# How E and F reach a fused attention and MLP-mixer kernel on one core: two loads moved from GpSimd to SyncE, with their casts on ScalarE and VectorE

## The chip, the cores and the metric

The kernel runs on one core of one Trainium2 chip. The metric is device time in microseconds (us) of one execution. Beside the times there is one profiled execution: each instruction on TensorE (PE, with its weight loads as PEld), VectorE (DVE), ScalarE (ACT) and GpSimd (POOL), the DMA instructions that POOL and SyncE (SP) issue, and the packets that the core's 16 DMA engines moved.

## The reference

```python
k_proj = einsum('ks,bhsd->bhkd', E, k)          # q, k, v: 8 batches, 8 heads, 1024 rows, 64 columns
v_proj = einsum('ks,bhsd->bhkd', F, v)          # E, F: 64 x 1024
scores = softmax(q @ k_proj^T / sqrt(64))       # 1024 x 64 for each head
x = (scores @ v_proj), heads side by side       # 8 x 1024 x 512
h = relu(x^T @ w_tok1) @ w_tok2                 # 1024 -> 256 -> 1024, over the rows
u = x + h^T
out = u + relu(u @ w_ch1) @ w_ch2               # 512 -> 1536 -> 512
```

All inputs and the output are f32 in DRAM. On the chip the products run in bf16. Everything that uses k or v needs E or F first, so these two matrices (256 KB each in f32) stand at the head of the computation.

## The kernel before, in words

The program treats the eight batches one after another and mixes the instructions of neighbouring batches. Each step has a short name, and a list `ORDER`, written out by hand, gives the order in which the steps are written to the engines; each engine then runs its own instructions in that order. `ON_DVE` names the copies that go to DVE; the others go to ACT.

Loads are issued by POOL (`nc.gpsimd.dma_start`), because they cast f32 to bf16 on the way. POOL's instructions also run in the order in which they stand, so a load waits for all that POOL has to do ahead of it. The order at the start is: E (L197) and F (L198) into the two halves of the tile `EF_sb`, 64 partitions each; then, for each of the four pairs of heads of batch 0, a load of k, of q and of v (`load`, L165, 256 KB each as bf16), with `make_identity` (a memset and a select on POOL, masks.py:197 and 199) after the v load of the first pair; then `wt1` (L206), `wt2` (L207), the channel weights (L191, L195) and q, k and v of batch 1.

On PE the start is as follows. `busy(c_ps, 8)` runs eight matmuls on a tile of zeros (L226); their product isn't used. Step `EF` (`eft`, L228 to L232) turns `EF_sb` with eight transposes, which need `EF_sb` and `ident`, and DVE copies the result to `EFT`. Step `KP.0` multiplies `EFT` with k of the first pair of heads (L240), `QT.0` transposes q (L395), `VP.0` multiplies with v (L245), and so on for the pairs 1, 2 and 3, in the order that the first lines of `ORDER` give:

```python
EF KP.0 Ka.0 W1 KT.0 Ba.0 Bd.0 QT.0 KP.1 QC.0 VP.0 Ka.1 S1.0 QT.1 KT.1 QC.1 VP.1 lv2 Bd.1 Ba.1
Vd.0 KP.2 S0.0 Va.0 E1.0 Vd.1 O1.0 Ka.2 QT.2 Va.1 KT.2 S0.1 E0.0 S1.1 E1.1 QC.2 Ba.2 Bd.2 O0.0
```

`W1` is three more matmuls on zeros, and `KP.1`, `KP.2`, `KP.3` and `VP.3` begin with four, two, two and three matmuls of the same kind (`FILL`, L431). S and E are scores and exponentials, O is the product with v, M and N are the two token products (L464, L477). After about 35 us the channel products of batch 0 follow (L532), and from batch 1 on they are done with seven products of half-size blocks where eight would be plain (L600, L655).

SP issues the transposing DMAs of q and u (L178, L362) and the stores of the output (L676, L680) from the f32 tiles `o1` and `o2`, of two buffers each. It issues nothing in the first 70 us.

## Time and profile before

| What | Value |
|---|---|
| time, three runs | 430.47, 430.73, 430.92 us |
| profiled execution | 430.72 us, of which the trace spans 428.9 us from its first to its last instruction |
| PE busy in the span | 416.0 us (97%) |
| DVE, ACT, POOL busy | 302.0, 202.4, 205.7 us |
| granted TensorE clock | 0.999 |
| moved by POOL's DMA queue | 29.63 MB as they land (bf16), 43.9% of 16 engines' span |
| moved by SP's DMA queue | 30.42 MB, 29.6% |

The busy share of PE is an average over the whole span, and it counts matmuls that wait in the pipeline. The stage that the change touches is the first of the profile's 40 slices, each of 10.7 us. The bytes of a load that casts are counted as they land, so 205 GB/s of landed bf16 stand for 410 GB/s read from DRAM.

### The profile page before, as it was taken

How to read it: one execution, taken by the hardware profiler on the slowest of the kernel's cores; microseconds unless marked ns; L12 is line 12 of the kernel's file. 1: busy time of each engine (PE TensorE's matmuls, PEld its weight loads, DVE VectorE, ACT ScalarE, POOL GpSimd, SP SyncE). 2: the span in 40 equal slices, each digit the busy share in tenths (PEclk: the TensorE clock that was granted, in tenths of full speed). 3: DMA queues.
4: the chain of work that ended last, by engine and by line, in shares of the span. 5: the costliest groups of instructions: out<-in, count | busy, mean ns of one | idle time of the engine just before them, and what ended most of it. 6: DMA issues, size and time to landing. Idle time of an engine off the chain costs nothing.

```text
span 428.9 us, 7732 instructions
## 1 busy us (share of the span) xinstructions
PE 416.0 (97%) x3066; PEld 271.0 (63%) x3066; DVE 302.0 (70%) x509; ACT 202.4 (47%) x360; POOL 205.7 (48%) x150
## 2 busy tenths in 40 slices
PE   6799999999999999999999999999999999999995
PEld 3486456765478644785467744786458854785585
DVE  2575568768836878867768777777779766947862
ACT  1446684167553556234753365334652356215621
POOL 8350024135563547552565645635456626654652
PEclk9999999999999999999999999999999999999999
DMA  8999999879996999943999279364914320342014
GB/s 128 207 202 206 207 205 183 208 128 223 194 124 172 171 222 184 178 81 70 253 164 203 114 132 160 66 169 113 147 36 105 92 99 2 60 140 98 2 50 147
DMA packets 89332, 60.53 MB, mean 141 GB/s; under 512 B 55760, under 2 KB 84944, under 8 KB 89296
## 3 DMA queue, kind: packets, MB, share of 16 engines
q0 software_dynamic: 29360, 29.63, 43.9%
q1 hardware_dynamic: 59936, 30.42, 29.6%
q8 instruction: 24, 0.39, 0.4%
q14 instruction: 12, 0.10, 0.1%
HBM read 59.24 MB, written 16.78 MB: 177 GB/s over the span
## 4 chain that ended last, share of the span: by engine, by line
PE 91%; DVE 4%; DMA 2%; POOL 2%; issue 0%; ACT 0%; DVEq 0%; ACTq 0%; POOLq 0%
PE be L655 19%; PE be L600 17%; PE ga L655 9%; PE ga L600 8%; PE h_ps L341 6%; PE u_ps L357 5%; PE g_ps L532 5%; PE al L655 4%; PE al L600 4%; PE ou_ps L294 4%; PE kv_ps L240 3%; PE sco L281 3%; DMA q_sb<-in_q_dram 2%; DVE S L524 1%; PE u_ps L477 1%; PE h_ps L464 1%
## 5 line engine op out<-in xcount | busy, mean ns | idle before, releaser
L564 ACT ACTIVATE K<-be 128x512 f32<-128x512 f32 x116 | 65.7, 598 | 66.2 <-PE be L655 39.4
L655 PEld LDWEIGHTS <-g 128*128 128x128 bf16 x768 | 74.5, 98 | 16.2 <-issue 1.0
L655 PEld LDWEIGHTS <-S 128*128 128x128 bf16 x576 | 55.9, 98 | 11.7 <-issue 0.4
L286 ACT ACTIVATE attnT<-sco 128x512 bf16<-128x512 f32 x56 | 33.5, 598 | 50.8 <-PE sco L281 50.7
L600 PEld LDWEIGHTS <-wc 128*128 128x128 bf16 x336 | 32.1, 98 | 36.1 <-DVE g L606 0.4
L691 POOL TENSOR_TENSOR K<-K,u_sb 128x512 f32<-128x512 f32 x16 | 19.0, 1185 | 68.5 <-ACT K L564 68.5
L655 PE MATMUL be<-wc,g 128*128 128x256 bf16 x384 | 48.5, 273 | 0.6 <-DVE g L522 0.6
L564 ACT ACTIVATE K<-ga 128x512 f32<-128x512 f32 x58 | 33.0, 601 | 33.6 <-PE ga L655 29.9
L301 DVE TENSOR_TENSOR x_sb<-ou_ps,rdn 128x512 bf16<-128x512 f32 x64 | 44.3, 692 | 2.2
L600 PE MATMUL be<-uT,wc 128*128 128x512 bf16 x168 | 44.7, 379 | 0.0
L360 DVE TENSOR_TENSOR u_sb<-u_ps,x_sb 128x512 bf16<-128x512 f32 x56 | 37.1, 684 | 9.4 <-PE u_ps L357 8.9
L600 PEld LDWEIGHTS <-uS 128*128 128x128 bf16 x252 | 24.0, 98 | 25.7
L606 DVE CUSTOM_DVE_ANT_0 g<-be,K 128x512 bf16<-128x512 f32 x42 | 27.5, 688 | 16.8 <-PE be L600 16.6
L518 POOL TENSOR_TENSOR S<-g 128x1024 bf16<-128x1024 bf16 x7 | 14.8, 2121 | 47.0 <-DVE g L606 47.0
L522 POOL TENSOR_TENSOR g<-g 128x1024 bf16<-128x1024 bf16 x13 | 28.9, 2226 | 14.8 <-DVE S L518 14.6
L639 ACT ACTIVATE g<-be 128x512 bf16<-128x512 f32 x42 | 23.8, 597 | 25.7 <-PE be L600 25.7
L606 DVE CUSTOM_DVE_ANT_0 g<-al,K 128x512 bf16<-128x512 f32 x42 | 27.7, 688 | 10.7 <-PE al L600 10.4
L701 POOL TENSOR_TENSOR K<-K,u_sb 128x512 f32<-128x512 f32 x16 | 20.0, 1247 | 30.0 <-ACT K L564 30.0
L357 PE MATMUL u_ps<-R_sb,wt 128*128 128x512 bf16 x112 | 31.0, 379 | 0.3 <-DVE u_sb L360 0.3
L300 DVE RECIPROCAL rdn<-ou_ps 128x8 f32<-128x8 f32 x64 | 13.1, 205 | 25.8 <-PE ou_ps L294 25.4
L341 PE MATMUL h_ps<-x_sb,wt 128*128 128x512 bf16 x112 | 29.9, 379 | 0.0
L524 POOL TENSOR_TENSOR S<-g,S 128x1024 bf16<-128x1024 bf16 x13 | 28.4, 2185 | 0.9 <-ACT K L564 0.7
(101 smaller groups left out, 777.1 us busy)
## 6 DMA issues: line engine op xcount, KB each, us to landing
out_dram<-o SPq DMA_DIRECT2D x30, 512.0 KB, 3.0
q_sb<-in_q_dram POOLq DMA_DIRECT2D x7, 1024.0 KB, 13.0
k_sb<-in_k_dram POOLq DMA_DIRECT2D x7, 1024.0 KB, 11.5
v_sb<-in_v_dram POOLq DMA_DIRECT2D x7, 1024.0 KB, 13.4
wc<-in_moe_w_ch_dram POOLq DMA_DIRECT2D x4, 384.0 KB, 14.3
wc<-in_moe_w_ch_dram POOLq DMA_DIRECT2D x2, 768.0 KB, 27.7
k_sb<-in_k_dram POOLq DMA_DIRECT2D x4, 256.0 KB, 7.0
q_sb<-in_q_dram POOLq DMA_DIRECT2D x4, 256.0 KB, 7.6
```

What stands on the lines that cost most here:

```text
L286: nc.scalar.activation(out=at, in_=sco, func=ACT.Exp, scale=scale)
L301: nc.vector.tensor_tensor(out=st["x", b][:, :, h * D : (h + 1) * D].rearrange("p (b k) d -> p b k d", b=2), in0=ov[:, :, :, 0:D], in1=rdn[ ...
L341: nc.tensor.matmul(st["h", b], wt1[:, s, t * P : (t + 1) * P], st["x", b][:, s, :], start=(s == 0), stop=(s == SC - 1),)
L357: nc.tensor.matmul(u_ps, wt2[:, t, s::SC], st["R", b][:, t, :], start=(t == 0), stop=(t == TC - 1))
L360: nc.vector.tensor_add(out=st["u", b][:, s, :], in0=u_ps, in1=st["x", b][:, s, :])
L522: eng.tensor_sub(out=a21, in0=a11, in1=a21)
L524: eng.tensor_sub(out=s4, in0=a12, in1=s2)
L564: nc.scalar.activation(out=t, in_=x, func=ACT.Copy)
L600: nc.tensor.matmul(acc, l[:, dc, i * P : (i + 1) * P], r[:, :, dc, :], start=start and dc == 0, stop=stop and dc == 1, skip_group_check=True,)
L606: nc.vector._custom_dve(TENSOR_ADD_SAT, out=o, in0=x, in1=y, s0=3.0e38, s1=0.0)
L639: nc.scalar.activation(out=g_part(b, i + e, 1, 1, 0)[:, 0], in_=be[e], func=ACT.Relu)
L655: nc.tensor.matmul(acc[:, e * HF : (e + 1) * HF], l[:, lc + c, l0 + (2 * j + e) * P : l0 + (2 * j + e + 1) * P], r[:, rc + c, r0 : r0 + HF ...
```

## The change

E and F are no longer loaded by POOL with a cast. SP loads them as f32 into a new tile `EF_in`, which takes a buffer of the tag `o1`. ACT then casts columns 0 to 511 into `EF_sb` and DVE columns 512 to 1023. POOL's first instruction of the kernel's body is now the load of k of the first pair of heads, followed by q, then `make_identity`, then v and all the rest in the old order. On ACT the cast stands ahead of all its other work, behind the load of its function table; on DVE it stands after the four memsets and ahead of the copy to `EFT`. On PE nothing is added, removed or moved.

```diff
-    nc.gpsimd.dma_start(out=EF_sb[0:KP], in_=E)
-    nc.gpsimd.dma_start(out=EF_sb[KP:P], in_=F)
+    EF_in = work.tile([P, S], F32, tag="o1", name="EF_in", bufs=2)
+    nc.sync.dma_start(out=EF_in[0:KP], in_=E)
+    nc.sync.dma_start(out=EF_in[KP:P], in_=F)
     for hp in range(HP):
         hs = slice(2 * hp, 2 * hp + 2)
         for name, src in ((("k", k), ("q", q), ("v", v))):
             load(0, name, src, hs)
-        if hp == 0:
-            make_identity(nc, ident)
+            if (hp, name) == (0, "q"):
+                make_identity(nc, ident)
...
     busy(c_ps, 8)
+    nc.scalar.activation(out=EF_sb[:, 0 : S // 2], in_=EF_in[:, 0 : S // 2], func=ACT.Copy)
+    nc.vector.tensor_copy(out=EF_sb[:, S // 2 : S], in_=EF_in[:, S // 2 : S])
```

## The prediction

> **What bounds the kernel now.** The page's slices come first, to see which stage differs from the rest:

> ```profile
> ## 2 busy tenths in 40 slices
> PE   6799999999999999999999999999999999999995
> ...
> GB/s 128 207 202 206 207 205 183 208 128 223 194 124 172 171 222 184 178 81 70 253 164 203 114 132 160 66 169 113 147 36 105 92 99 2 60 140 98 2 50 147
> ```

> PE is full from slice 3 on. Only in slices 1 and 2 (0 to 21 us) does it have gaps, and there the DMAs run at some 205 GB/s as soon as they have begun. The chain that ended last, from its start, says who sets the pace there:

> ```profile
> 1.24 0.69 POOL EF_sb L197
> 1.93 0.52 POOL EF_sb L198
> 2.46 0.57 POOL k_sb L165
> ...
> 4.63 0.23 POOL ident masks.py:197
> ...
> 8.02 8.45 DMA q_sb<-in_q_dram
> 16.47 0.04 issue
> 16.51 0.62 PE qt_ps L395 x8
> ```

> Columns are start, length, what. The chain is POOL issuing loads, then the DMA queue until q of pair 2 lands at 16.47, then PE (with short DVE pieces) to the end. The waits of the window 5 to 17 us agree: PE waits for loads.

> ```profile
> PE kv_ps L240 <- DMA k_sb<-in_k_dram: 2.5, 2, 1.6
> ...
> PEld L231 <- DMA EF_sb<-in_E_dram: 0.9, 1, 0.9
> PEld L240 <- DVE EFT L232: 0.9, 1, 0.9
> PEld L395 <- DMA q_sb<-in_q_dram: 0.7, 2, 0.4
> ```

> The 2.5 us are KP.0 (waits 1.64, starts 7.57) and KP.1 (waits 0.88, starts 11.38). The loads' issue to landing, from the list of DMA issues in short windows, is 5.1, 5.6, 6.2 (k, q, v of pair 0), 6.2, 6.8, 7.3 (pair 1), 7.9 and 8.4 (k and q of pair 2). With the starts of the issues they land at 7.57, 8.8, 10.1, 11.4, 12.7, 13.9, 15.2 and 16.5: one each 1.27 us. 256 KB in 1.27 us is 206 GB/s, so this is a full stream, and what matters is when it becomes full. The stretches of the start (last number: GB/s) show that:

> ```profile
> 3.25:4.50 1.25, 1.25 (x5) 0.34 (x3) 0.00 (x0) 0.00 (x0) 1.25 (x2) 1.00 1.03 190
> 4.50:4.75 0.25, 0.25 (x2) 0.00 (x0) 0.00 (x0) 0.00 (x0) 0.25 (x2) 1.00 0.45 37
> 4.75:5.50 0.75, 0.53 (x5) 0.37 (x5) 0.00 (x0) 0.00 (x0) 0.68 (x3) 1.00 0.87 98
> 5.50:7.50 2.00, 0.43 (x7) 0.40 (x6) 0.69 (x1) 0.00 (x0) 2.00 (x4) 1.00 1.20 195
> ```

> E and F (256 KB landed) fill 3.25 to 4.5. Then the engines run dry to 37 GB/s: k's packets aren't there yet. They begin near 4.7, some 1.4 us after k's issue ended at 3.18, as E's began near 3.25, 1.3 us after its issue ended at 1.93. So k isn't held up by the bytes of E and F but by the time POOL takes to issue them.

> [...] The trace agrees as to what is at stake (0.69 + 0.52 us of POOL, and a dry spot behind it); how a SP load beside POOL's stream fares, it doesn't show. [...]

> **The change part by part.**
> POOL's queue. Two issues go, 0.69 + 0.52 = 1.21 us. k of pair 0 is issued at 1.24 where it was 2.45, q at about 1.97, then identity (4.60 to 5.17 before, so 0.57 us) at about 2.7, done by 3.3 where it was 5.2. v comes at 3.3 (before 3.89) and all later issues 1.2 us sooner. v gains only 0.6, but its packets (end of issue 4.0 plus 1.4 = 5.4) are there before k and q have streamed through (3.3 plus 2 x 1.27 = 5.8), so the stream stays full. Issues from v of pair 3 on wait for landings (0.5 to 0.7 us each) and move with these. POOL's stream moves 1.2 us. Bounds: the first DMA may pay E's extra (0.69 against F's 0.52) on top, so 1.05; the slow start at 4.75 to 5.50 (98 for 205 GB/s, 0.75 x 107/205 = 0.39 us) may vanish behind other traffic, so 1.6.

> SP's two loads, not in the trace. Nearest row: the last four stores (L676, SP, 256 KB of f32 each), issued in 0.38 us, with packets moving from 0.9 to 1.6 us after the issue and landing after 2.3. SP has nothing queued ahead; behind these, its first work is at 70 us. It passes the start barrier like DVE, whose first memset is at 0.92; I take E's issue at 1.0 and F's at 1.4. Packets then move from 1.9 to about 3.4 and land at 3.3 and 4.1. I add 0.4 for cold first packets: F at 4.5. Bounds of F: 3.7 without barrier delay, and with the longest landing of SP's stores (8.1, L680) 9.5. In DMA time the 512 KB cost, at 410 GB/s, 1.28 us; nearly all of it lies before POOL's packets at 3.3. I charge the stream 0.1 for the overlap; bounds 0 and 1.28.

> The casts. ACT: a 128x512 f32 activation took 598 ns (L564, from PSUM). [...] ACT is idle from its table load (ends 2.77) to 9.13, DVE from 2.24 to 5.97. Behind the DVE cast stands only the copy to EFT, which needs it anyway, and behind ACT's only the copy at 9.13. [...] EF_sb is ready at 4.5 + 0.6 = 5.1.

> PE. Its eight zero matmuls end at 5.05, as before, so the transposes start at about 5.1 (5.27 before), end 5.8, the EFT copy (0.69) ends 6.5, and KP.0 can start at 6.5. k lands at 7.57 - 1.1 = 6.5. KP.0 gains 1.1. From KP.0 to the end of KP.1's four fills took 2.94 us (7.57 to 10.51), so KP.1 is ready at 9.45 and waits for k of pair 1 at 11.38 - 1.1 = 10.3. F may be 0.8 us later than I took before KP.1 feels it.

> What follows. KP.1 to QT.2 wait for loads and move with them. After 16.5 us the order is fixed and each piece is released by PE or DVE; wt1 lands at 24.7 for M1.0 at 25.25, wt2 at 27.1 for N1.0 at 28.37, v of batch 1 at 50.5 for a product at 51.1: all in POOL's stream, all shifting with it. Nothing there takes time back or gives more. `EF_in` is read long before `o1` is first written: 0.

> The sum: -1.21 + 0.1 = -1.1 us on the span of 428.9, and the same on the time: the profiled run had 430.72, the median of the three is 430.73. 430.7 - 1.1 = 429.6.

> **The rivals.**
> More gain: E and F wholly ahead of the stream and the slow start gone as well, -1.21 - 0.39 = -1.6, with 0.2 more if the dry 0.25 us was part of it: 428.9 to 429.1. For it: the dry spot; against it: some cold start stays.
> No change: E and F as f32 on the same engines take their 1.28 us out of POOL's stream, which eats the 1.21: 430.7; half of it gives 430.1. For it: the stream is full at 205 GB/s; against it: that only begins after 3.3 us, and SP can begin sooner. That the change doesn't do what it says ends here too: POOL may reach its first load no sooner than 2 us.
> Slower: F lands late. EFT is then the bound: F + 0.6 + 0.7 + 0.7 gives KP.0, + 2.94 KP.1, so F + 5.0. It decides from F at 5.3 on, gives no net gain at 6.4, and at 9.5 puts KP.1 at 14.5, 3.1 late, of which 0.8 us of PE gaps up to QT.2 take a part: +2.3, so 433.0; F at 8.5 gives 432.0. For it: 8.1 us did occur on SP's queue[...]. Against it: that was a store in a busy stretch, here the engines are empty.

> **How the numbers follow.** The stream moves by POOL's issue time: 0.62, with 429.3 to 430.0 as its own range; more gain 0.12; eaten 0.18 (430.0 to 430.7); late F 0.08. 0.2%, about what can be told from no change, is 0.86 us, so "faster" ends at 429.87. That takes 0.54 of the first case and all of the second, 0.66; the rest of the first and the third are "same", 0.26; late F is "slower", 0.08. The range 428.9 to 430.6 leaves out late F, the far end of the eaten case and a little of the large gain.

> **What would show it.** KP.0 (L240 of before) near 6.5 in place of 7.57, KP.1 near 10.3 in place of 11.38, QT.2 near 15.4 in place of 16.51, M1.0 near 24.1; no dry stretch once POOL's packets have begun; SP's loads landed by 4.5. The forecast is wrong if PE waits for EF_sb beyond 5.8, if k lands at 7.4 or later, or if QT.2 gains 1.1 us and the gain is gone by 50 us.

## The result, and the profile after

| | Median (runs) | Profiled span | Share of granted clock |
|---|---|---|---|
| before | 430.60 us (4: 430.43 to 430.92) | 428.9 us | 0.999 |
| after | 433.49 us (4: 433.27 to 433.81) | 431.5 us | 0.992 |

The ratio is 1.0067, with a 95% interval of 1.0049 to 1.0084. The change makes the kernel 2.9 us slower. The forecast was 1.1 us faster, with a range that ended at 430.6.

The slices of the page of after:

```profile
## 2 busy tenths in 40 slices
PE   4989999999999999999999999999999999999996
...
PEclk8899999999999999999999999999999999999999
...
GB/s 167 209 191 199 207 164 182 191 160 199 202 116 193 159 220 185 187 99 43 248 163 218 81 161 156 84 171 84 174 37 79 117 99 2 51 147 97 2 50 146
```

The first slice moves more (167 GB/s, before 128), but 0.26 of the 0.43 MB that it moves more are E and F themselves, which now land as f32 (the page of before has 59.24 MB read from HBM for the 29.63 MB, as bf16, that POOL's queue landed). That the loads behind them start sooner shows in the table below. PE works less in it (4, before 6), and `PEclk` has an 8 in slices 1 and 2 where before had none. The chain that ended last, at its start, columns as before:

```profile
0.74 0.58 SPq L198
1.38 4.83 DMA EF_in<-in_F_dram
6.37 1.21 issue
7.58 0.64 ACT EF_sb L236
8.26 1.09 PE e_ps L232 x8
9.37 0.70 DVE EFT L233
10.12 1.06 PE kv_ps L243 x8
11.18 1.39 PE w_ps L227 x3
12.79 0.97 PE qt_ps L398 x8
13.76 1.51 PE kv_ps L434 x4
15.27 0.40 PE kv_ps L243 x5
```

Before, this chain ran through POOL's issues to q of pair 2. Now it runs through F and then through PE alone: PE never again waits for a load of batch 0. F lands at 6.2. The "issue" of 1.21 us behind it is on ACT, and ACT's timeline tells what it is:

```profile
6.28 1.28 ACT L236 ACT_TABLE_LOAD   x1 [6.28 <-DMA EF_in<-in_F_dram]
7.58 0.63 ACT L236 ACTIVATE EF_sb<-EF_in 128x512 bf16<-128x512 f32 x1
```

The load of ACT's function table now waits for F (the bracket tells the releaser), and in the kernel before it didn't, as its timeline shows:

```profile
1.49 1.28 ACT L249 ACT_TABLE_LOAD   x1 [1.49 <-DVE kbd L216]
```

The cast needs both E and F; E had landed at 4.4, and ACT sat idle for 6.3 us until F. Before, the first ACT instruction of the body ran at 9.13, behind PE, but its table load was released by the memset at 1.49.

Then the clock. The stretches of after, cut where its clock changes; the third number from the end is the granted clock:

```profile
4.70:8.11 3.41, 0.24 (x1) 0.00 (x0) 0.43 (x1) 1.82 (x2) 3.41 (x6) 1.00 1.18 194
8.11:11.52 3.41, 2.48 (x18) 1.79 (x19) 0.99 (x2) 0.10 (x1) 2.43 (x4) 0.50 1.24 204
11.52:14.93 3.41, 3.41 (x17) 1.56 (x15) 0.81 (x2) 0.54 (x2) 1.59 (x3) 0.50 1.24 205
14.93:18.34 3.41, 3.41 (x44) 2.26 (x43) 1.38 (x4) 1.53 (x4) 1.18 (x2) 1.00 1.24 205
```

From 4.94, where the zero matmuls end, to 8.26 PE has nothing to do, and from 8.11 to 14.93 it runs at half clock. Up to 4.70 there is no clock record; the eight zero matmuls take 3.48 us there, which is about the pace of half clock (the three of `W1` take 1.46 us at half clock here and 0.82 at full clock before). The transposes of E and F take 1.07 us in place of 0.66, KP.0 1.06 in place of 0.61, the four fills of KP.1 1.71 in place of 1.03. Before:

```profile
5.27 0.66 PE L231 MATMUL e_ps<-ident,EF_sb 128*128 128x128 bf16 x8 [0.22 <-POOL ident masks.py:199]
7.57 0.61 PE L240 MATMUL kv_ps<-k_sb,EFT 128*64 128x128 bf16 x8 [1.64 <-DMA k_sb<-in_k_dram]
9.48 1.03 PE L431 MATMUL kv_ps<-EFT,ident 128*128 128x512 bf16 x4
```

After:

```profile
8.26 1.07 PE L232 MATMUL e_ps<-ident,EF_sb 128*128 128x128 bf16 x8 [3.32 <-ACT EF_sb L236]
10.12 1.06 PE L243 MATMUL kv_ps<-k_sb,EFT 128*64 128x128 bf16 x8 [0.78 <-DVE EFT L233]
13.55 1.71 PE L434 MATMUL kv_ps<-EFT,ident 128*128 128x512 bf16 x4
```

| Step (start, us) | before | forecast | after |
|---|---|---|---|
| k of pair 0 lands | 7.5 | 6.5 | 6.5 |
| k of pair 1, q of pair 2 land | 11.3, 16.5 | 10.3, 15.4 | 10.4, 15.6 |
| F lands | 5.0 | 4.5 | 6.2 |
| transposes of E and F | 5.27 | 5.1 | 8.26 |
| KP.0 | 7.57 | 6.5 | 10.12 |
| KP.1 | 11.38 | 10.3 | 15.20 |
| QT.2 | 16.51 | 15.4 | 19.07 |

QT.2 is 2.56 us late and the span 2.6 us longer: what is lost in the first 19 us is never given back, and nothing is lost after it.

### The profile page after: what moved, and what is told of

It reads as the page before. It is cut to its first block, busy times and chain, and to the rows that moved or that the text cites. A ratio compares the mean times of both kernels' runs of the same rounds, so it can differ in the third digit from the quotient of the medians.

```text
span 431.5 us, 7738 instructions
## 1 busy us (share of the span) xinstructions
PE 418.2 (97%) x3066; PEld 271.8 (63%) x3066; DVE 301.4 (70%) x510; ACT 202.9 (47%) x361; POOL 205.2 (48%) x148
## 3 DMA queue, kind: packets, MB, share of 16 engines
HBM read 59.24 MB, written 16.78 MB: 176 GB/s over the span
## 4 chain that ended last, share of the span: by engine, by line
PE 92%; DVE 4%; DMA 1%; issue 1%; ACT 0%; POOL 0%; SPq 0%; ACTq 0%; DVEq 0%
PE be L658 19%; PE be L603 17%; PE ga L658 9%; PE ga L603 8%; PE h_ps L344 6%; PE u_ps L360 5%; PE g_ps L535 5%; PE al L658 4%; PE al L603 4%; PE ou_ps L297 4%; PE kv_ps L243 4%; PE sco L284 3%; DMA EF_in<-in_F_dram 1%; DVE S L527 1%; PE qt_ps L398 1%; PE u_ps L480 1%
## 5 line engine op out<-in xcount | busy, mean ns | idle before, releaser
L609 DVE CUSTOM_DVE_ANT_0 g<-be,K 128x512 bf16<-128x512 f32 x42 | 27.3, 687 | 17.1 <-PE be L603 16.1
L525 POOL TENSOR_TENSOR g<-g 128x1024 bf16<-128x1024 bf16 x13 | 29.0, 2235 | 14.7 <-DVE S L521 14.5
L609 DVE CUSTOM_DVE_ANT_0 g<-al,K 128x512 bf16<-128x512 f32 x42 | 27.6, 687 | 11.2 <-PE al L603 11.0
## 6 DMA issues: line engine op xcount, KB each, us to landing
q_sb<-in_q_dram POOLq DMA_DIRECT2D x7, 1024.0 KB, 11.4
wc<-in_moe_w_ch_dram POOLq DMA_DIRECT2D x4, 384.0 KB, 13.4
```

The lines of the kernel that those rows point to most:

```text
L525: eng.tensor_sub(out=a21, in0=a11, in1=a21)
L609: nc.vector._custom_dve(TENSOR_ADD_SAT, out=o, in0=x, in1=y, s0=3.0e38, s1=0.0)
```

## The experiments

My theory before the first run: three things add up, F lands late, the table load follows it, and PE's clock falls in the gap. The rivals were the late F alone, the clock alone, and a stream of loads that gives nothing. All kernels compute the reference in full; zero matmuls and helper tiles aren't part of the result. Each ratio is to the kernel before on the same chip, whose median there was 431.46 to 431.54. The profile of a run is one of its executions; "full clock from" is the time from which PE keeps full clock in it (5.22 in the kernel before, 14.93 in after); where no clock record stands ahead of it, half clock is read from the length of the matmuls (in e6_before_cold KP.0 took 1.06 us for 0.61).

| Run | Median, us | Ratio to before (95%) | KP.0, KP.1, QT.2 in the profile | Full clock from |
|---|---|---|---|---|
| r_after: the change again | 433.61 | 1.0047 (1.0029 to 1.0065) | 10.86, 15.60, 19.46 | 14.98 |
| e1_table | 432.10 | 1.0009 (0.9996 to 1.0021) | 8.48, 13.51, 17.38 | 13.20 |
| e4_dve_cast | 431.80 | 1.0000 (0.9988 to 1.0012) | 8.94, 13.85, 17.72 | 13.42 |
| e2_warm | 431.34 | 1.0004 (0.9993 to 1.0015) | 9.55, 12.44, 16.31 | 5.32 |
| e3_table_warm | 430.90 | 0.9984 (0.9970 to 0.9999) | 9.35, 12.24, 16.11 | 7.09 |
| e9_one_queue | 430.26 | 0.9983 (0.9965 to 1.0002) | 8.26, 11.15, 15.61 | 5.21 |
| e5_two_queues | 429.82 | 0.9966 (0.9957 to 0.9974) | 8.41, 11.31, 15.68 | 4.78 |
| e11_dve_12 | 431.01 | 0.9996 (0.9977 to 1.0015) | 9.31, 14.58, 18.85 | 15.50 |
| e6_before_cold | 431.47 | 0.9998 (0.9989 to 1.0007) | 7.07, 11.74, 16.19 | 11.07 |
| e10_before_12 | 431.30 | 0.9997 (0.9988 to 1.0006) | 7.25, 11.95, 17.08 | 5.03 |
| e8_pool_late | 431.47 (one run) | - | 7.90, 11.73, 16.95 | 5.68 |

**The change again.** 

> The changed kernel once more, on the chip of the next runs, to compare these with. My theory has a part that depends on when PE's clock windows (3.41 us in the clock records of the runs so far) fall against the start, so the size may vary from run to run: 432.0 to 434.0, slower than before by 1 to 3 us. If the loss were in the waits alone it would repeat at 433.5.

It repeats: 433.26 to 433.79 in four runs, 2.1 us over before. F landed later still, at 7.0, and here k of pair 1 landed at 11.3 and q of pair 2 at 16.4, as in the kernel before. So how much POOL's stream gains varies as well. Of the nine profiles in which POOL begins with k at once, k of pair 1 landed at 10.4 to 10.8 in six and at 11.2 to 11.3 in three (r_after, e4_dve_cast, e11_dve_12). With E and F on POOL it landed at 11.0 (e6_before_cold), 11.3 (before) and 11.9 (e10_before_12).

**The table load.** e1_table puts this ahead of ACT's cast:

```diff
+    first = const.tile([P, 1], BF16, name="first")
+    nc.scalar.activation(out=first, in_=kbd[:, 0, 0:1], func=ACT.Copy)
```

> The changed kernel with one small activation on zeros ahead of ACT's cast, so that the table load (1.28 us) waits for a memset and not for F. If the late F, the table load behind its wait and a half clock on PE add up (my theory), the cast ends near 6.9 in place of 8.21, PE idles some 1.9 us in place of 3.3 and keeps its clock, KP.1 comes near 11.4 in place of 15.2, and the time is 429.8 to 430.8. If the late F alone costs it, the time stays within 0.3 of the change's 433.5. If PE's clock falls in any case, 431.5 to 432.5.

The table was loaded at 0.74, and ACT's cast came right behind F (5.93 to 6.56). The change's loss was mostly gone, 0.6 us over before where r_after was 2.1 over, but I had expected more: PE's gap was cut to 1.57 us, and still it ran at half clock until 13.2. So the time is that of the third expectation, though in the profile the clock didn't fall: it was never granted before 13.2. The single runs lie far apart, from 430.6 to 433.0. e4_dve_cast comes to the same by another way; DVE casts all 1024 columns (0.69 us) and ACT none:

```diff
-    nc.scalar.activation(out=EF_sb[:, 0 : S // 2], in_=EF_in[:, 0 : S // 2], func=ACT.Copy)
-    nc.vector.tensor_copy(out=EF_sb[:, S // 2 : S], in_=EF_in[:, S // 2 : S])
+    nc.vector.tensor_copy(out=EF_sb, in_=EF_in)
```

> The changed kernel with the whole cast of 1024 columns on DVE (about 0.8 us by the 0.43 of 512 columns) and none on ACT, so that no table load stands behind a wait for F. My theory: EF_sb near 7.1, as in the run with the early table load plus 0.2, so 430.0 to 431.0. If ACT's table load doesn't matter, 433 or more.

EF_sb was ready at 7.03, as expected, but PE was at half clock until 13.4, and 431.80 is 0.8 us over my range: a miss for the same reason.

**The clock.** e2_warm leaves the table load where the change has it and only keeps PE busy:

```diff
-    busy(c_ps, 8)
+    busy(c_ps, 22)
```

> The changed kernel with 22 zero matmuls at the start in place of 8, so that PE is busy until about 8; EF_sb is as late as in the change (8.2). If PE's half clock between 8.3 and 15.2 us is over half of the loss, as I hold, KP.0 comes near 9.7, KP.1 near 12.7, and the time is 430.4 to 431.4. If the lateness of EF_sb is what costs, and the clock only goes with it, the time stays at 433.0 to 433.6.

KP.1 is at 12.44 and the loss is gone from the median, though the transposes begin at 8.11, hardly sooner than in the change (8.26). Fifteen of the 20 runs took 430.7 to 431.8; the other five, all with a clock share of 0.996, took 432.7 to 433.3, and when their clock was lost is not on record. Keeping the clock thus takes the loss away where it succeeds, and the early table load took 1.6 of its 2.1 us. The two are not parts of a sum, because the clock cost time only together with the late E and F: e6_before_cold (431.47 against 431.48) takes the clock from the kernel before, with `busy(c_ps, 1)`:

> The kernel before with 1 zero matmul at the start in place of 8: nothing else is changed, so PE meets EF and KP.0 to KP.1 at half clock while loads and EFT are on time. My theory prices the half clock at some 2.2 us between EF and KP.1, of which KP.0's wait hides 0.4 and KP.1's wait 0.9, and later waits up to 0.8: KP.1 near 12.4, QT.2 0 to 0.6 late, time 0.0 to 0.8 over before. If PE's clock is granted late by the first matmuls in any case, no difference at all; if half clock alone explains the change's loss, 2 us over before.

PE in the profile of e6_before_cold (start, length, instruction):

```profile
5.27 1.01 PE L231 MATMUL e_ps<-ident,EF_sb 128*128 128x128 bf16 x8 [3.20 <-POOL ident masks.py:199]
7.07 1.06 PE L240 MATMUL kv_ps<-k_sb,EFT 128*64 128x128 bf16 x8 [0.79 <-DVE EFT L232]
8.06 1.46 PE L226 MATMUL w_ps<-kbd 128*128 128x512 bf16 x3
...
11.74 0.47 PE L240 MATMUL kv_ps<-k_sb,EFT 128*64 128x128 bf16 x5
```

The same slow matmuls, and the time stays at 431.47 against 431.48: QT.2 still starts with the landing of its q (16.1), because the waits for loads, 1.64 and 0.88 us in the kernel before, take up what the clock costs. (In this profile q of pair 2 landed 0.3 us sooner than in the profile of before; the medians are of 12 and 24 runs.) In the change PE runs behind the loads, and nothing takes it up. This is why the rival "the clock alone" falls too.

**Both remedies.** e3_table_warm has the table load early and 17 zero matmuls:

> The changed kernel with both: the table load early and 17 zero matmuls. Only the late F remains (landed near 6.2). My theory: KP.0 near 8.4, KP.1 near 11.3, then loads that are some 1 us sooner than before the change, so 429.5 to 430.3, a little under the kernel before. A rival by which POOL's earlier stream gives nothing: 430.5 or more.

It is under before, but the zero matmuls themselves, at half clock until 7.09, ended only at 8.06 and held up the transposes (7.90, with E and F cast since 6.5). So KP.1 came 0.9 us later than I had expected, and 430.90 lies in the range of the rival, a stream that gives nothing; this run doesn't decide between them. With 12 zero matmuls they end near 6. e9_one_queue has 12 and the early table load:

> As the run with E and F on two queues, but both issued by SP again: the changed kernel with the table load early and 12 zero matmuls. The two queues did not bring E and F in sooner (6.1), so this should be the same as that run: KP.0 near 8.4, KP.1 near 11.3, 1.0 to 1.8 us under before. If the second queue was what made it faster, no better than before.

e5_two_queues has that and issues F from ACT in place of SP:

```diff
-    nc.sync.dma_start(out=EF_in[KP:P], in_=F)
+    nc.scalar.dma_start(out=EF_in[KP:P], in_=F)
```

> The changed kernel with F issued by ACT's own DMA queue beside E on SP's, the table load early and 12 zero matmuls. If F is late because it is issued 0.64 us behind E on one queue, it lands near 5.5 in place of 5.9 to 6.3, KP.0 near 7.8, KP.1 near 10.8, and the time is 0.5 to 1.2 under before. If F is late because the same 16 DMA engines share out E, F and k, it lands at 5.8 or later and the time is as with the early table load and 17 zero matmuls, 0 to 0.8 under before.

The later of the two matrices landed at 6.1 (E; F at 4.8), not sooner than 6.0 in e9_one_queue, so here the second queue only changes which one is last, and in the profiles both kernels are alike. The time is lower than either of my cases had it. The chain of e5_two_queues is the one that I had forecast for the change:

```profile
1.24 0.48 POOL k_sb L165
...
6.91 8.72 DMA q_sb<-in_q_dram
15.63 0.05 issue
15.68 0.62 PE qt_ps L400 x8
```

QT.2 is 0.83 us earlier than before and waits for its load again. At 429.82 us, 0.34% under the kernel before, this version beats both kernels; the interval of e9_one_queue still reaches 1.0002. The runs of e9_one_queue spread more: the eight with a clock share of 0.998 and up took 429.5 to 430.7 us, two with 0.995 took 431.0 and 431.4, two with 0.992 took 432.7 and 433.7. A lost window of 3.41 us at half clock is 0.004 of the share (3.41 x 0.5 / 430), and the profile of after, with two, has 0.992; so these fit runs in which the clock fell for one or two windows; the share doesn't say when. None of the 13 runs of e5_two_queues is under 0.998; why it keeps the clock more often than e9_one_queue isn't settled. In the kernel before, beside these, the share doesn't tell the time: 15 runs at 0.996 and under took 430.6 to 432.3, 13 above it 430.3 to 432.1. That agrees with e6_before_cold.

e11_dve_12 joins the cast on DVE with 12 zero matmuls:

> The changed kernel with the whole cast on DVE (0.70 us) and 12 zero matmuls. EF_sb is ready some 0.1 to 0.2 later than with the split cast behind an early table load, which KP.1 feels and the loads of pair 2 hide: 0.8 to 1.8 under before, by the same two remedies without a helper activation. If PE's gap of some 0.5 us more lets the clock fall, 0 to 1 over before.

In its profile F landed at 7.0, the gap behind the zero matmuls was 1.7 us, and the clock fell; that run has a share of 0.992 and took 433.1, with two windows at half clock (8.67 to 15.50). Runs at 0.998 and up took 429.7 to 430.3, three at 0.995 431.0 to 431.5, the three at 0.992 near 433: the same steps as in e9_one_queue. The median is a miss against my 0.8 to 1.8 under. Twelve zero matmuls bridged to an F at 6.0 (e9_one_queue), not at 7.0 (here).

**Controls.** e10_before_12 gives the kernel before the 12 zero matmuls:

> The kernel before with 12 zero matmuls in place of 8. Control for the runs with 12: if their gain comes from POOL's loads being about 1 us sooner, this stays within 0.4 of before (PE has over 1 us to spare ahead of KP.1). If a steadier clock is what gains, it is 1.0 to 1.8 under before as well.

No change, so the gain of e5_two_queues isn't the zero matmuls' own. That it is POOL's earlier stream, e8_pool_late supports: with 8 zero matmuls and the table load early, POOL's k of pair 0 is held back from 1.24 to 2.95 by four memsets of a scratch tile.

```diff
+    hold = const.tile([P, 512], F32, name="hold")
+    for _ in range(4):
+        nc.gpsimd.memset(hold, 0.0)
```

> The changed kernel with the table load early and four memsets of a scratch tile ahead of POOL's first load, so that k of pair 0 is issued some 2 us later and the loads of E and F have the DMA engines to themselves. If sharing with k's packets is what delays F, F lands near 4.7 to 5.2 in place of 5.9 to 6.3. If SP's queue or cold DRAM is slow by itself, F lands at 5.8 or later as before. The time isn't the point: the stream of loads is late, 431 to 433.

Its span is 429.7 us where the profile of e9_one_queue has 427.9, with full clock from 5.68 and 5.21. The issue is 1.7 us later, QT.2 1.3 us (16.95, with the landing of its q at 16.9, for 15.61); what makes up the rest of the 1.8 us is open, and it is a single execution. Its main question was F. The list of DMA issues of e8_pool_late:

```profile
EF_in<-in_E_dram SPq DMA_DIRECT2D x1, 256.0 KB, 3.9
EF_in<-in_F_dram SPq DMA_DIRECT2D x1, 256.0 KB, 4.3
```

F, issued at 1.38, lands at 5.6 with the DMA engines nearly to E and F alone, between my two cases; in the other kernels on SP it landed at 5.5 to 7.0. So 1.1 us of F's lateness against my 4.5 is there without POOL's packets. That sharing with POOL makes the rest, up to 1.3 us, is not shown: e2_warm has F at 5.5 beside POOL's packets. The stretches show how the two loads move:

```profile
2.00:2.50 0.50, 0.50 (x3) 0.17 (x2) 0.13 (x2) 0.23 (x2) 0.44 (x2) 1.00 1.13 131
2.50:3.00 0.50, 0.50 (x2) 0.15 (x1) 0.00 (x0) 0.00 (x0) 0.50 (x2) 1.00 0.60 246
3.00:3.50 0.50, 0.50 (x2) 0.15 (x1) 0.00 (x0) 0.00 (x0) 0.50 (x2) 1.00 1.15 320
3.50:4.00 0.50, 0.50 (x3) 0.15 (x2) 0.00 (x0) 0.00 (x0) 0.50 (x2) 1.00 1.15 270
4.00:4.50 0.50, 0.50 (x3) 0.15 (x1) 0.00 (x0) 0.00 (x0) 0.50 (x1) 1.00 0.37 74
```

They begin at 131 GB/s (the first packet at 2.10), reach 320 only after 1 us, and their last packets come slowly again, at 74 GB/s after 4.0. The stores from which I took the duration moved at 332 and 348 GB/s in the half microseconds that fell wholly inside one. What limits the beginning and the end is open.

## Why the prediction was wrong

**Right: POOL's queue.** "POOL's stream moves 1.2 us", less 0.1, measured 0.9 in after (k of pair 1 at 10.45 for 11.34), and k landed at 6.5, as forecast. It was worth about what I said once nothing else stood in the way: e5_two_queues is 1.5 us under before (430 x 0.0034), and the one run of e8_pool_late doesn't have it. Its spread was missed: in three of nine profiles the stream gained 0.1 us or nothing.

**Wrong: the terms on the way of E and F.** My own sign of a wrong forecast, PE waiting for EF_sb beyond 5.8, came true: it waited until 8.26. I had KP.1 ready at 9.45; it was at 15.20. The 5.75 us are four terms of that sum:
- F's landing, 6.2 for 4.5: +1.7. The nearest row was a store at the end of the kernel; a load at the very start was slower by itself (5.6 in e8_pool_late), and in most profiles slower still beside k (up to 7.0). The 0.4 us that I added for the first packets was my own allowance.
- "ACT is idle from its table load (ends 2.77)": +1.4. This step failed outright. The instruction that I put first on ACT took the table load with it behind its wait, so EF_sb came 2.0 us after F and not 0.6. ACT's cast was as priced, 0.63 us for 0.6; DVE's took 0.43, of a form that no row of the trace of before has. I took the cast's duration and the engine's idle time, without asking which wait its table load would inherit.
- Transposes and EFT copy, 1.9 for 1.4: +0.5, nearly all half clock.
- "From KP.0 to the end of KP.1's four fills took 2.94 us": +2.1, it took 5.08. I carried over a duration from a profile with full clock, without asking what PE's gap does to the clock.

The last two are one missed resource, PE's clock. The trace of before held two signs of it that I didn't use: its eight zero matmuls at the start took 3.59 us (0.45 each) where the three of `W1`, of the same shape, took 0.82 (0.27 each); and at its end, where PE's last matmul ends at 424.6, the clock is at half from 428.47. In the runs the clock records change in steps of 3.41 us (in after it falls at 8.11 and is back at 14.93, two steps later), and where the steps lie against the start of the kernel differs: the cuts are at 4.70, 4.78, 5.21 and 5.68 in four profiles (after, e5_two_queues, e9_one_queue, e8_pool_late).

**The rivals.** "Slower: F lands late" was the right place with the wrong point. It was to decide from F at 5.3 on and to bring no loss before 6.4. With F at 6.2 the change should have been no slower; e9_one_queue, F at 6.0, shows that this part was right, with KP.1 at 11.15 for my F + 5.0. In the change KP.1 was F + 9.0. Of the 3.8 us that KP.1 is late, 1.26 came back up to QT.2 (15.20 to 19.07 for 11.38 to 16.51); I had 0.8. "No change", E and F eating up POOL's gain, fits the loads of the three profiles without a gain, but it isn't what made the kernel slower.

## What to carry to other kernels

F could land 1.0 us later than before at no cost (e9_one_queue), because loads kept PE waiting anyway, until the delay let PE's clock fall; then the matmuls up to the next grant took up to 1.8 times as long (in after 1.46 us for 0.82). Before an instruction is put first on ACT, look at what its table load will wait for, and give the table load an instruction of its own that has nothing late to wait for: behind one that needed only a memset it ran at 0.74 (e1_table; 0.73 in e9_one_queue), behind one that needed E and F at 6.28 (after). Taking two loads off POOL's queue was worth up to the time of their issue there (1.21 us; k of pair 1 landed 0.9 us sooner in after), but the landing of a load at the start of a kernel has to come from a load there, not from a store at the end: priced from such a store F was to land at 4.5, and it landed at 6.2.

## What the runs showed of the hardware that was not expected

```profile
5.22:8.63 3.41, 1.72 (x19) 1.29 (x19) 1.11 (x2) 0.00 (x0) 3.41 (x5) 1.00 1.17 190
```

```profile
5.26:8.67 3.41, 1.54 (x12) 0.78 (x10) 0.80 (x2) 0.00 (x0) 3.35 (x5) 1.00 1.14 187
```

From these two, 1.72 us and kept, 1.54 us and lost, my estimate is that the kernel before is itself some 0.2 us of work away from the fall, which would fit that 48 of its 94 runs beside the experiments have a share of 0.996 or less. The matmuls' ends are modelled, and 2.79 and 2.78 can't be told apart, so these numbers only part the cases seen here; that the busy time is what decides is my inference from them, which no run tests by itself. The share of granted clock didn't count the time before the first grant: e6_before_cold has 0.999 with full clock only from 11.07. So a high share doesn't mean a kept clock: one run of r_after has 0.998 and took 433.79.
